# Masking the top-k scores with ScalarE's parametric ReLU, splitting the normalization, and transposing one turn sooner

## The chip, the cores and the metric

The kernel runs on one core of a Trainium2 chip. The core has a matrix engine (TensorE, PE in the profile, with its weight loads shown as PEld), a vector engine (VectorE, DVE), an activation engine (ScalarE, ACT), a general engine (GpSimd, POOL), and a queue that issues transfers (SyncE, SP). Each engine works through its own instructions in order; engines wait for each other through semaphores. The metric is the device time of one execution in microseconds (us).

## What is computed

An attention block with 8 batches, 8 heads, 576 positions and 64 columns a head, where each query keeps only its 32 largest scores, is followed by a SwiGLU feed-forward block on 4608 tokens of 512 columns with 1536 hidden columns. All is fp32.

```python
scores = scale * np.matmul(q, k.transpose(0, 1, 3, 2))          # scale = 1/8
kth = np.partition(scores, -top_k, axis=-1)[..., -top_k:-top_k + 1]
scores = np.where(scores >= kth, scores, -1000000000.0)
attn = np.exp(scores - np.max(scores, axis=-1, keepdims=True))
attn = attn / (np.sum(attn, axis=-1, keepdims=True) + 1e-09)
x = matmul(attn, v)                        # (B,H,S,D) -> (B*S, H*D)
g = x @ w_gate
out = (g * (1.0 / (1.0 + np.exp(-g))) * (x @ w_val)) @ w_out
```

## The kernel before

**Units and turns.** The attention work is cut into 160 units: batch (8), query tile (five, of 128 queries; the last has 64 queries of each head of a pair, stacked to 128 rows), and pair of heads (4). Units of the first four tiles handle two heads, [128 queries, 576 keys] each; units of the last tile hold both heads of the pair as one [128, 576] tile, and are half as much work. One pass of the main loop (L747) is called a turn; turn n carries out the selection of unit n on DVE and, around it, other steps of neighbouring units. A batch is 20 turns: 16 whole and 4 half ones.

**What happens to a unit.** `scores` (L278) multiplies q and k on PE into PSUM and copies the result to SBUF on ScalarE (`sc`, L313 or L299). `select` (L316) finds the 32 largest scores of each row on DVE: four rounds of `max` (eight values each, L328) with three `match_replace` between them (L332, which overwrites the values found, in `e`). That makes 14 instructions for two heads, which the text calls steps. Then L338 builds in `e` a penalty: (score < 32nd value) times a huge negative number. `penalize` (L342), on GpSimd, makes the bias from the largest value (L348) and adds the scores to the penalty (L350), one instruction a head. `weigh` (L353), on ScalarE, takes the exponential with the row sum as a by-product (L359) and adds 1e-9 to the sum (L364). `normalize` (L367) takes the reciprocal on DVE (L371) and multiplies each head by it on ScalarE (L374). `turn` (L376) transposes `e` on PE, nine blocks of up to 128 columns (L386), and copies them out on ScalarE (`et`, L387). The middle block of the nine holds columns of both heads. `values` (L398) multiplies by V on PE for two units at a time (L420) and copies the result into `xT` on ScalarE (L436).

**When.** In turn n: `penalize` and `weigh` of unit n-1; the reciprocal of n-1 at the turn's end, and its two multiplications at the beginning of turn n+1 (`scaled`); the transposes of unit n-2 (`TURN = 2`), behind up to two pieces of feed-forward work. In even turns the scores of units n+1 and n+2 are made and the V products of n-4 and n-3 (`scored` and `valued`, L708 and L713); the second score product is issued behind the V products, its copies behind `weigh`. In the first turns `rounding` works on the weights: a transfer, three ScalarE instructions (L114 to L117), one on DVE (L121) and two on GpSimd (L122, L123) for each of 36 pieces.

**Feed-forward work.** The tokens are taken in 18 blocks of 256 rows. A block may start when `values` has finished its rows for all four head pairs. `feed` (a generator) yields it in pieces: a piece of the first layer is four matrix products, eight records in the trace (L476), and costs 1; a piece of the second layer, three products (L562), costs 0.75. ScalarE evicts the gate (L501 to L503) and the value (L508), GpSimd multiplies them (L504, L509). From the second block on the second layer is done with seven products of quarters and additions on GpSimd (L548, L569 to L610). `share` (L694) gives each turn a credit: 6.4 pieces for a whole turn, less 0.7 for every unit whose scores or V products are made in it, less 0.6 for the transposes. `pieces(k)` issues up to k pieces if the credit lasts, at five places of the turn: 2 early, 1 and 1 around the middle, up to 6 at the end; what ScalarE and GpSimd owe for them is issued at the next `flush`.

**Order.** The last lines of the kernel tie each engine's instructions to the order in which the program wrote them. Nothing is rearranged: where one waits, all behind it on that engine wait. PSUM holds five banks for scores, V products and transposes (`ps_t`) and three for the feed-forward work.

```python
        if nxt:
            run(nxt.pop(0))
        if valued(n):
            finish_units(valued(n))
        if nxt:
            next(nxt[0])
        early[0]()
        if 0 <= n - 1 < NU:
            weigh(n - 1)
        if nxt:
            run(nxt.pop())
```

Of the kernel before, what the change touches and what calls it, by code (L numbers as in the profile page):

```python
# [8 lines left out]
AF = mybir.ActivationFunctionType  # L9
ALU = mybir.AluOpType  # L10
FP32 = mybir.dt.float32
# [4 lines left out]
P = 128  # L16
TOP_K = 32
LOWEST = -3.4028234663852886e38
FAR = -3.0e38
EPS = 1.0e-9  # L20
BLK = 256
WP = 256
# [3 lines left out]
def kernel(  # L26
# [66 lines left out]
    for i in range(NV):  # L93
        vt = consts.tile([P, P], FP32, name=f"vlast{i}")
        nc.vector.memset(vt[:], 0.0)
        vlast.append(vt)
    eps = consts.tile([P, 1], FP32, name="eps")
    nc.vector.memset(eps[:], EPS)
    wg = consts.tile([P, KC, DFF], FP32, name="wg")
    wv = consts.tile([P, KC, DFF], FP32, name="wv")  # L100
    wo = consts.tile([P, MC, DM], FP32, name="wo")
# [176 lines left out]
    def scores(n):  # L278
        b, qt, hp = units[n]
        slab = preps[b * NHP + hp]  # L280
        sc = work.tile([P, 2 * S], FP32, tag="sc", name="sc", bufs=3)
        halves = [slice(0, D), slice(D, P)]
        half = S // 2

        def bank():
            return ps_t.tile([P, 512], FP32, tag="t", name="s")


        if qt == J:
            banks = [bank() for _ in range(2)]  # L290
            for i, ps in enumerate(banks):
                for d in halves:
                    k0 = R + i * half
                    nc.tensor.matmul(  # L294
                        ps[d, 0:half], slab[d, S + R : S + 2 * R], slab[d, k0 : k0 + half]
                    )
            yield
            for i, ps in enumerate(banks):
                nc.scalar.copy(sc[:, i * half : (i + 1) * half], ps[:, 0:half])  # L299
        else:  # L300
            q0 = S + 2 * R + qt * P
            banks = []
            for i in range(2):
                for hh, d in enumerate(halves):
                    ps = bank()
                    banks.append((i + 2 * hh, ps))
                    k0 = (1 - hh) * R + i * half
                    nc.tensor.matmul(  # L308
                        ps[:, 0:half], slab[d, q0 : q0 + P], slab[d, k0 : k0 + half]
                    )  # L310
            yield
            for i, ps in banks:
                nc.scalar.copy(sc[:, i * half : (i + 1) * half], ps[:, 0:half])  # L313
        state[n] = dict(sc=sc)

    def select(n):  # L316

        nh = n_heads(units[n][1])
        sc = state[n]["sc"]
        m = small.tile([P, 2, TOP_K], FP32, tag="m", name="m", bufs=2)  # L320
        heads = [slice(t * S, (t + 1) * S) for t in range(nh)]
        e = work.tile([P, 2 * S], FP32, tag="e", name="e", bufs=3)
        state[n] |= dict(m=m, e=e, heads=heads)
# [2 lines left out]
        for r in range(rounds):  # L326
# [3 lines left out]
            if r < rounds - 1:  # L330
# [3 lines left out]
                    )  # L334
                    yield
                cur = e
        for t, hs in enumerate(heads):
            nc.vector.tensor_scalar(  # L338
                e[:, hs], sc[:, hs], m[:, t, TOP_K - 1 : TOP_K], FAR, ALU.is_lt, ALU.mult
            )  # L340

    def penalize(n):  # L342

        st = state[n]
        sc, m, e, heads = st.pop("sc"), st.pop("m"), st["e"], st["heads"]
        nh = len(heads)
        bias = small.tile([P, 2], FP32, tag="bias", name="bias")
        nc.gpsimd.tensor_scalar_mul(bias[:, 0:nh], m[:, 0:nh, 0], -scale)  # L348
        for hs in heads:
            nc.gpsimd.tensor_tensor(e[:, hs], e[:, hs], sc[:, hs], ALU.add)  # L350
        st["bias"] = bias

    def weigh(n):  # L353

        st = state[n]
        e, heads, bias = st["e"], st["heads"], st.pop("bias")
        tot = small.tile([P, 2], FP32, tag="tot", name="tot")
        for t, hs in enumerate(heads):
            nc.scalar.activation(  # L359
                e[:, hs], e[:, hs], AF.Exp, bias=bias[:, t : t + 1], scale=scale,  # L360
                accum_out=tot[:, t : t + 1],
            )
        nh = len(heads)
        nc.scalar.activation(tot[:, 0:nh], tot[:, 0:nh], AF.Identity, bias=eps[:])  # L364
        st["tot"] = tot

    def normalize(n):  # L367
        st = state[n]
        tot, e, heads = st.pop("tot"), st["e"], st.pop("heads")
        nh = len(heads)  # L370
        nc.vector.reciprocal(tot[:, 0:nh], tot[:, 0:nh])  # L371
        yield
        for t, hs in enumerate(heads):
            nc.scalar.mul(e[:, hs], e[:, hs], tot[:, t : t + 1])  # L374

    def turn(n):  # L376

# [329 lines left out]

    def scored(n):  # L708

        ahead = [n + 1] if n < 2 else [] if n % 2 else [n + 1, n + 2]  # L710
        return [m for m in ahead if m < NU]

    def valued(n):  # L713

        behind = [] if n % 2 else [n - 4, n - 3]
        return [m for m in behind if 0 <= m < NU]

    def pieces(n):
# [4 lines left out]
    def run(steps):  # L723
        for _ in steps:
            pass
# [15 lines left out]
    load(2)  # L741
    credit = [0.0]
    no = iter(())
    scaled = no
    TURN = 2
    due = [2.0]
    for n in range(NU + 3):  # L747
        nh = n_heads(units[n][1]) if n < NU else 1
# [17 lines left out]
            credit[0] = min(credit[0] + share(n), share(n) + 1)  # L766
        flush(on_act)
        if 0 <= n - 1 < NU:
            penalize(n - 1)
        flush(on_pool)  # L770
        run(scaled)
        if nxt:
            run(nxt.pop(0))
        if valued(n):
# [18 lines left out]
        flush(on_act)  # L793
        dve(1)
        dve(1)
        if 0 <= n - TURN < NU:
            run(turn(n - TURN))

        flush(on_pool)
        next(ahead, None)  # L800
        pieces(1)
        next(ahead, None)
        dve(1)
        pieces(1)
        dve(2, beside=False)
        run(topk)
        next(norm, None)
        scaled = norm
        pieces(6)
    while piece():  # L810
        pass
# [48 lines left out]
```

## Time and profile before

| | |
|---|---|
| median of 3 runs (lowest, highest) | 1791.11 us (1789.26, 1791.48) |
| the profiled execution | 1790.76 us, its span 1788.7 us |
| mean granted TensorE clock | 0.966 of full |
| L328 and L332, selection on DVE | 614.5 + 202.5 and 423.3 + 211.5 us |
| L338, penalty on DVE | 185.4 us, 288 instructions |
| L350, adding the scores on GpSimd | 408.7 us, 288 instructions, 1437 ns each |
| L359, exponential on ScalarE | 222.8 us, 288 instructions, 778 ns each |
| L374, normalization on ScalarE | 210.9 us, 288 instructions, 781 ns each |
| L386, transposes on PE | 184.0 us, idle before them 45.7 us |

A busy time is the union of an engine's instructions; "mean ns" is the length of one, which overlaps with its neighbour's. The slices cut the span into 40 equal parts and give each engine's busy share in tenths. Matrix products are pipelined and their ends are modelled, so a full PE need not be at its highest rate; its rate is read from the distance of one product to the next. In timelines a line gives start, length, engine, line, operation, operands (out<-in), number of instructions, and in brackets the idle time before it with what ended it.

### The profile page before, as it was taken

The page shows a single profiled execution, that of the slowest core. Times are in us where ns is not written, and L with a number is a line of the kernel's source. Part 1 is how long each engine was busy: PE and PEld are TensorE (multiplying, and loading weights), DVE is VectorE, ACT ScalarE, POOL GpSimd, SP SyncE. Part 2 cuts the span into 40 slices and gives each one's busy share as a digit, 9 for nine tenths or more (in the row PEclk, how much of TensorE's full clock was granted, in tenths as well). Part 3 has the DMA queues.
Part 4 walks back from the last instruction along what each step waited for, and adds up shares of the span by engine and source line. Part 5 has one row for each costly group of instructions (what it writes and reads, how often), then busy time and mean ns, then how long its engine had stood idle before and what let it go on. Part 6 is the DMA issues. An engine that isn't in the chain of part 4 may idle for free.

```text
span 1788.7 us, 30860 instructions
## 1 busy us (share of the span) xinstructions
PE 1686.3 (94%) x11012; PEld 1396.2 (78%) x11012; DVE 1619.7 (91%) x3372; ACT 1209.5 (68%) x2881; POOL 1068.0 (60%) x1058
## 2 busy tenths in 40 slices
PE   4458999799999999999999999999999999999999
PEld 3337678588888888888888878888888878888877
DVE  7999999999999999999999989999999999999400
ACT  6788776667667677667666776767676776676431
POOL 4878856455565646564656646566556555756434
PEclk7669999899999999999999999999999999999989
DMA  7433030001200030001200030000300020000000
GB/s 193 126 96 95 32 75 14 13 1 36 60 1 13 3 80 15 12 1 35 62 13 1 13 71 26 1 13 6 90 1 13 1 55 15 13 1 13 1 12 12
DMA packets 109306, 59.67 MB, mean 33 GB/s; under 512 B 88544, under 2 KB 96992, under 8 KB 109152
## 3 DMA queue, kind: packets, MB, share of 16 engines
q1 hardware_dynamic: 108016, 57.37, 12.3%
q8 instruction: 87, 1.43, 0.3%
q14 instruction: 67, 0.55, 0.1%
q10 hardware_dynamic: 1136, 0.33, 0.1%
HBM read 48.23 MB, written 9.44 MB: 32 GB/s over the span
## 4 chain that ended last, share of the span: by engine, by line
PE 81%; DVE 9%; POOL 4%; ACT 3%; issue 2%; DMA 0%; SPq 0%; POOLq 0%; ACTq 0%; DVEq 0%
PE f L476 39%; PE x_ps L562 9%; PE av L420 8%; PE s L308 7%; PE etps L386 6%; PE y_ps L562 6%; DVE m L328 4%; DVE e L332 4%; PE s L294 2%; POOL e L350 1%; PE kqps L263 1%; PE o_ps L522 1%; DVE e L338 1%; DVE size L121 1%; ACT e L359 1%
## 5 line engine op out<-in xcount | busy, mean ns | idle before, releaser
L328 DVE MAX8 m<-e 128x8 f32<-128x576 f32 x864 | 614.5, 746 | 3.3
L350 POOL TENSOR_TENSOR e<-e,sc 128x576 f32<-128x576 f32 x288 | 408.7, 1437 | 111.8 <-DVE e L338 53.8
L332 DVE MATCH_REPLACE8 e<-m,e 128x576 f32<-128x576 f32 x576 | 423.3, 741 | 0.0
L476 PE MATMUL f<-xT,wg 128*128 128x256 f32 x1728 | 405.6, 384 | 0.0
L476 PE MATMUL f<-xT,wv 128*128 128x256 f32 x1728 | 399.6, 380 | 0.0
L476 PEld LDWEIGHTS f<-xT,wg 128*128 128x128 f32 x1728 | 326.4, 192 | 52.2 <-issue 8.9
L476 PEld LDWEIGHTS f<-xT,wv 128*128 128x128 f32 x1728 | 323.0, 190 | 49.1 <-issue 7.9
L504 POOL TENSOR_TENSOR h<-h,half_g 128x512 f32<-128x512 f32 x108 | 139.0, 1287 | 284.1 <-ACT h L503 274.5
L359 ACT ACTIVATE e<-e,bias 128x576 f32<-128x576 f32 x288 | 222.8, 778 | 79.0 <-POOL e L350 79.0
L509 POOL TENSOR_TENSOR h<-h,val 128x512 f32<-128x512 f32 x108 | 139.4, 1291 | 148.7 <-ACT val L508 147.9
L386 PE MATMUL etps<-ident,e 128*128 128x128 f32 (+1 forms) x1312 | 184.0, 284 | 45.7 <-ACT e L374 37.5
L374 ACT ACTIVATE e<-e,tot 128x576 f32<-128x576 f32 x288 | 210.9, 781 | 20.9 <-DVE tot L371 20.8
L308 PE MATMUL s<-kqT 64*128 64x288 f32 x1024 | 181.4, 461 | 41.9 <-ACT sc L313 27.6
L386 PEld LDWEIGHTS etps<-ident,e 128*128 128x128 f32 (+1 forms) x1312 | 157.5, 145 | 76.6 <-ACT e L374 41.4
L387 ACT COPY et<-etps 128x512 f32<-128x512 f32 (+1 forms) x448 | 182.5, 483 | 44.1 <-PE etps L386 44.0
L332 DVE MATCH_REPLACE8 e<-m,sc 128x576 f32<-128x576 f32 x288 | 211.5, 740 | 0.0
L328 DVE MAX8 m<-sc 128x8 f32<-128x576 f32 x288 | 202.5, 739 | 9.1 <-ACT sc L313 9.1
L338 DVE TENSOR_SCALAR e<-sc,m 128x576 f32<-128x576 f32 x288 | 185.4, 680 | 1.1
L313 ACT COPY sc<-s 128x288 f32<-128x288 f32 x512 | 164.9, 407 | 17.0 <-PE s L308 16.8
L308 PEld LDWEIGHTS s<-kqT 64*128 64x128 f32 x1024 | 102.6, 198 | 89.6 <-ACT sc L313 33.0
L420 PE MATMUL av<-et,v 128*64 128x128 f32 (+1 forms) x2560 | 158.6, 267 | 0.0
L501 ACT ACTIVATE h<-f 128x512 f32<-128x512 f32 x108 | 64.3, 595 | 116.8 <-PE f L476 116.6
(73 smaller groups left out, 2045.9 us busy)
## 6 DMA issues: line engine op xcount, KB each, us to landing
v<-in_v_dram SPq DMA_DIRECT2D x32, 256.0 KB, 3.2
kq_in<-in_k_dram SPq DMA_DIRECT2D x63, 128.0 KB, 2.9
kq_in<-in_q_dram SPq DMA_DIRECT2D x63, 128.0 KB, 3.1
w<-in_moe_w_gate_dram SPq DMA_DIRECT2D x12, 512.0 KB, 3.9
w<-in_moe_w_val_dram SPq DMA_DIRECT2D x12, 512.0 KB, 3.7
w<-in_moe_w_out_dram SPq DMA_DIRECT2D x12, 512.0 KB, 3.6
out_dram<-o SPq DMA_DIRECT2D x38, 128.0 KB, 2.4
out_dram<-o SPq DMA_DIRECT2D x16, 256.0 KB, 2.4
```

The costliest lines, as they stand in the source:

```text
L308: nc.tensor.matmul(ps[:, 0:half], slab[d, q0 : q0 + P], slab[d, k0 : k0 + half])
L328: nc.vector.max(m[:, t, 8 * r : 8 * r + 8], cur[:, hs])
L332: nc.vector.match_replace(e[:, hs], m[:, t, 8 * r : 8 * r + 8], cur[:, hs], LOWEST)
L338: nc.vector.tensor_scalar(e[:, hs], sc[:, hs], m[:, t, TOP_K - 1 : TOP_K], FAR, ALU.is_lt, ALU.mult)
L350: nc.gpsimd.tensor_tensor(e[:, hs], e[:, hs], sc[:, hs], ALU.add)
L359: nc.scalar.activation(e[:, hs], e[:, hs], AF.Exp, bias=bias[:, t : t + 1], scale=scale, accum_out=tot[:, t : t + 1],)
L374: nc.scalar.mul(e[:, hs], e[:, hs], tot[:, t : t + 1])
L386: nc.tensor.transpose(ps[0:kl, c * P : (c + 1) * P], e[:, k0 : k0 + kl], ident[:])
L387: nc.scalar.copy(et[0:kl, c0 : c0 + cn, :], ps[0:kl, 0 : cn * P].rearrange("p (c j) -> p c j", c=cn),)
L420: nc.tensor.matmul(av[d, i, 0:ql], weights_, moving, start=c == (0 if last else J), stop=c == (J if last else J - 1),)
L476: nc.tensor.matmul(ps[:, i, :], w[:, kc, m * P : (m + 1) * P], x[:, kc, :], start=(kc == 0), stop=(kc == KC - 1),)
L562: nc.tensor.matmul(ps, lhsT, T[i][m], start=m == 0, stop=m == MQ - 1)
```

## The change

1. **Mask.** L338 and L350 go. Scores are scaled by 1/8 when they are copied from PSUM. In `weigh`, ScalarE applies a parametric ReLU to (32nd value - score): a kept score gives a value of zero or below, which is multiplied by 2^-90; a lower score stays as it is. The exponential then multiplies by -2^90, so that a kept score gives (score - 32nd value) and the others overflow to an exponential of zero. The bias is (32nd value - largest), one GpSimd subtraction in `shift`, where `penalize` was.
2. **Sum and normalization.** The addition of 1e-9 goes from ScalarE to DVE, one instruction of one column for each head, ahead of the reciprocal. The first head is multiplied on ScalarE, the second on GpSimd.
3. **Order.** `normalize` of unit n-1 is run whole in turn n, after the eighth of DVE's 14 steps, and the transposes of unit n-1 follow in the same turn (`TURN = 1`), behind up to four pieces of feed-forward work where they stood behind two. Scores of n+1 and n+2 and V products of n-3 and n-2 are made in odd turns; they were made in even turns.
4. `m` has three buffers in place of two.

```diff
-FAR = -3.0e38
+SMALL = 2.0**-90
...
-    eps = consts.tile([P, 1], FP32, name="eps")
-    nc.vector.memset(eps[:], EPS)
...
-                nc.scalar.copy(sc[:, i * half : (i + 1) * half], ps[:, 0:half])
+                nc.scalar.mul(sc[:, i * half : (i + 1) * half], ps[:, 0:half], scale)
...
-        m = small.tile([P, 2, TOP_K], FP32, tag="m", name="m", bufs=2)
+        m = small.tile([P, 2, TOP_K], FP32, tag="m", name="m")
...
-        for t, hs in enumerate(heads):
-            nc.vector.tensor_scalar(
-                e[:, hs], sc[:, hs], m[:, t, TOP_K - 1 : TOP_K], FAR, ALU.is_lt, ALU.mult
-            )
-
-    def penalize(n):
+
+    def shift(n):
 
         st = state[n]
-        sc, m, e, heads = st.pop("sc"), st.pop("m"), st["e"], st["heads"]
-        nh = len(heads)
+        m, nh = st["m"], len(st["heads"])
         bias = small.tile([P, 2], FP32, tag="bias", name="bias")
-        nc.gpsimd.tensor_scalar_mul(bias[:, 0:nh], m[:, 0:nh, 0], -scale)
-        for hs in heads:
-            nc.gpsimd.tensor_tensor(e[:, hs], e[:, hs], sc[:, hs], ALU.add)
+        nc.gpsimd.tensor_tensor(
+            bias[:, 0:nh], m[:, 0:nh, TOP_K - 1], m[:, 0:nh, 0], ALU.subtract
+        )
         st["bias"] = bias
 
     def weigh(n):
 
         st = state[n]
-        e, heads, bias = st["e"], st["heads"], st.pop("bias")
+        sc, m, e, heads, bias = st.pop("sc"), st.pop("m"), st["e"], st["heads"], st.pop("bias")
         tot = small.tile([P, 2], FP32, tag="tot", name="tot")
         for t, hs in enumerate(heads):
             nc.scalar.activation(
-                e[:, hs], e[:, hs], AF.Exp, bias=bias[:, t : t + 1], scale=scale,
+                e[:, hs], sc[:, hs], AF.Prelu, bias=m[:, t, TOP_K - 1 : TOP_K], scale=-1.0,
+                alpha=SMALL,
+            )
+        for t, hs in enumerate(heads):
+            nc.scalar.activation(
+                e[:, hs], e[:, hs], AF.Exp, bias=bias[:, t : t + 1], scale=-1.0 / SMALL,
                 accum_out=tot[:, t : t + 1],
             )
-        nh = len(heads)
-        nc.scalar.activation(tot[:, 0:nh], tot[:, 0:nh], AF.Identity, bias=eps[:])
         st["tot"] = tot
 
     def normalize(n):
         st = state[n]
         tot, e, heads = st.pop("tot"), st["e"], st.pop("heads")
         nh = len(heads)
+        for t in range(nh):
+            nc.vector.tensor_scalar_add(tot[:, t : t + 1], tot[:, t : t + 1], EPS)
         nc.vector.reciprocal(tot[:, 0:nh], tot[:, 0:nh])
         yield
         for t, hs in enumerate(heads):
-            nc.scalar.mul(e[:, hs], e[:, hs], tot[:, t : t + 1])
+            if t == 0:
+                nc.scalar.mul(e[:, hs], e[:, hs], tot[:, t : t + 1])
+            else:
+                nc.gpsimd.tensor_tensor(
+                    e[:, hs], e[:, hs], tot[:, t : t + 1].to_broadcast([P, S]), ALU.mult
+                )
...
-        ahead = [n + 1] if n < 2 else [] if n % 2 else [n + 1, n + 2]
+        ahead = [n + 1, n + 2] if n % 2 else [] if n else [1]
...
-        behind = [] if n % 2 else [n - 4, n - 3]
+        behind = [n - 3, n - 2] if n % 2 else []
...
-    scaled = no
-    TURN = 2
+    TURN = 1
...
-            penalize(n - 1)
+            shift(n - 1)
         flush(on_pool)
-        run(scaled)
...
         flush(on_act)
         dve(1)
         dve(1)
-        if 0 <= n - TURN < NU:
-            run(turn(n - TURN))
-
+        run(norm)
         flush(on_pool)
         next(ahead, None)
         pieces(1)
         next(ahead, None)
         dve(1)
         pieces(1)
+        if 0 <= n - TURN < NU:
+            run(turn(n - TURN))
         dve(2, beside=False)
         run(topk)
-        next(norm, None)
-        scaled = norm
         pieces(6)
```

## The prediction

> **What bounds the kernel now.** I read busy shares and slices first, then windows, then one pair of turns instruction by instruction. A turn is one unit's top-32 selection on DVE. The page:
>
> ```profile
> PE 1686.3 (94%) x11012; PEld 1396.2 (78%) x11012; DVE 1619.7 (91%) x3372; ACT 1209.5 (68%) x2881; POOL 1068.0 (60%) x1058
> ...
> PE   4458999799999999999999999999999999999999
> ...
> DVE  7999999999999999999999989999999999999400
> ```
>
> PE and DVE are both full from slice 5 on, but DVE stops two slices before the end and PE does not. PE's 102.4 us of idle lie almost all at the start, as the windows show:
>
> ```profile
> 906.99:917.55 10.56, 10.56 (x55) 9.35 (x55) 10.56 (x25) 7.06 (x15) 5.93 (x7) 1.00 0.23 51
> ...
> 0.00:137.00 137.00, 67.46 (x364) 46.90 (x364) 125.06 (x260) 102.23 (x227) 96.40 (x85) 0.68 0.51 139
> ```
>
> (Columns: width, then busy PE, PEld, DVE, ACT, POOL with counts, granted clock, DMA.) Before 137 us PE idles 69.5 us because no FFN block is ready; in mid-kernel a turn of 10.56 us leaves neither PE nor DVE a gap. Is that PE at its rate? The chain in order of time has FFN products in a long run at
>
> ```profile
> 1659.06 13.82 PE f L476 x64
> ```
>
> 0.216 us a record, and in turns at 3.62 us for 16, the same once the modelled end is off. So PE's work (one "piece" of 8 records, 1.73 us, is its unit) fixes the middle; DVE is a close second. Cutting DVE there shortens nothing by itself; idle put into PE lengthens everything.
>
> **The change part by part.** The profiled execution took 1790.76 us (span 1788.7), 0.35 below the median 1791.11; the sum is made against 1790.8.
>
> *DVE.* Out go 288 mask instructions, L338, by the view of that line (min/median/max):
>
> ```profile
> L338 DVE TENSOR_SCALAR e<-sc,m x288: 490/512/1611, 23.0 to 1696.9; 128x576 f32<-128x576 f32 x144
> ```
>
> 185.4 us busy, about 53 of it above 0.46 each, the step of a pair (0.92). In come two one-column adds per turn; DVE has no such row. The nearest is L371, 128x2, 0.155 us long and 0.07 to the next instruction; I take 0.35 us for adds plus reciprocal (bounds 0.15 and 0.7). A DVE turn goes from 10.56 to about 10.0. L338's maximum is a stall: its long ones end some 0.32 us after a GpSimd instruction ends. If the adds stalled alike, by the mean of 53/288 = 0.18 us, a pair's loop below would gain 0.4 and the whole some 20 us. The sum takes none, since L371, the nearer in size, never exceeds 0.178. The Trainium skill (VectorE: DVE Perf Modes, What auto-detection actually checks) takes an fp32 instruction into its two-port mode only where an outermost dimension longer than one is even or equal; L338's 576 columns fit that and a lone column has no such dimension, so by the page too the 20 us would be nothing. No run here shows it yet.
>
> *ScalarE.* Two Prelu per turn come in, priced as L359 (0.78 alone, 1.44 for a pair as L374 x2; bounds 0.68, L117's, and 0.97, with L359's accumulator read): +1.44. One multiply of two goes (1.44 to 0.78) and L364 (0.30). Net +0.5 a turn, about 70 us on 1209: still under 75%. The scaling in the score copy is free if as L502 (594 ns) beside L508's copy (586). The trace has one table load of 1.283 us, at the start, and the changed program's ScalarE order also holds one, so the sum has nothing for tables. A rule against the change: by the Trainium skill (ScalarE: Activation LUTs, What ACT_TABLE_LOAD costs) each switch to another set of functions takes some 2.66 us, and a Prelu outside the set of Exp would mean two a turn, an estimated 850 us; no page says where Prelu lies, and the order decides.
>
> *GpSimd.* L350's 408.7 us go; 128 multiplies with a broadcast come, priced as L350 (1.437; a broadcast addition in L548 is 1377 against 1288 for 512 columns, so up to 1.53): +190. L348 becomes one subtraction of the same size. GpSimd is not the bound, but this multiply now stands between the reciprocal and PE.
>
> *The shorter chain.* This decides. Before, unit n-1 is normalized at the end of turn n and transposed in turn n+1, so PE finds e ready (waits of PE on L374: 79 us in all, counting weight loads twice). After, all is in turn n, with transposes behind the first pieces. From the changed order I list PE between V products: scores, V (two units), scores, 5.2 us of FFN, transposes, 6.9, transposes, 3.4. The typical odd-even pair of turns is PE time 4.67 + 15.5 + 1.96 = 22.1.
>
> The same pair is now also a loop of waits, since every engine keeps its order. From a pair before, on PE's and ScalarE's timelines:
>
> ```profile
> 897.61 1.24 PE L308 MATMUL s<-kqT 64*128 64x288 f32 x8
> ...
> 901.11 1.24 PE L308 MATMUL s<-kqT 64*128 64x288 f32 x8
> ```
>
> ```profile
> 901.23 0.37 ACT L436 COPY xT<-av 128x256 f32<-128x256 f32 x1 [1.53 <-PE av L420]
> 901.50 0.78 ACT L359 ACTIVATE e<-e,bias 128x576 f32<-128x576 f32 x1
> ```
>
> Counted from the odd turn's first score product: V is copied out and ScalarE free at 3.9. The two Prelu stand behind that copy: +1.33 (0.66 from one start to the next), then both Exp with accumulators +1.68 (923.04 to 924.72) = 6.9. DVE has stood at its adds since: done at 7.25. Six of its 14 steps remain (912.53 to 916.63): 4.1, so the next turn begins at 11.35. Eight steps (906.99 to 912.53): 5.54, adds and reciprocal 0.35 = 17.25. GpSimd's multiply 1.5 = 18.75, the five transposes of the second head 0.6 = 19.35. Then PE's FFN behind the even transposes, and the next pair starts. So a pair lasts the greater of PE time and 19.35 + that last FFN: 22.8 in the typical pair against 22.1.
>
> Over the changed order's 59 full pairs from turn 10 on: 32 pairs have about 3.4 us at the end (+0.93 each, 29.9); 14 have 5.3, mostly pairs of the second-layer quarters, whose calls are shorter so that more of them fall behind (+1.96, 27.5); 13 have under 2 (+1.56, 20.3). Together 77.7 us of PE idle, in place of about 20 (102.4, less 75.1 before 203.8 us and 7.5 after 1700): +58.
>
> Who waits: behind DVE's adds stand six selection steps, and ScalarE's next Prelu behind those; behind PE's transposes stand FFN products and the next scores. DVE's 3 to 4 us of waiting per pair costs only through the loop. The even turn's ScalarE chain (1.33 + 1.68) is hidden by DVE's eight steps (5.54); without that cover it would add up to 3 us a pair. In odd turns ScalarE multiplies head 0 only after the second scores' copies (1.28) and a value or gate eviction (0.6 or 1.6): 9.6 to 10.6 against PE's arrival at 9.85; that can cost 0 to 0.8 a pair, and I take 0 in the sum, since it is mostly absorbed in the loop.
>
> *Half turns (one head).* In the second pair of each batch PE reaches the odd transposes at 5.7 (4.67 + 1.0 of k/q transposes) but e is ready at about 7.7: 2 us, six or seven times, +12.
>
> *Start.* V two units earlier lets the first FFN block begin in turn 9 rather than 10: -11.5. The loop at the half clock (0.68 granted) with weight rounding on ScalarE makes a pair there some 25.5 against 24.94 (11.46 + 13.48): +2.5. Net -9; bounds -19 (DVE's saving comes through fully) and 0.
>
> *DMA.* V loads of the next batch and each output store are issued one turn sooner; DMA is 1 to 18% busy after 200 us, so 0. The queues on SP have nothing late behind them. *Tail:* one turn less latency, -2 (0 to -4).
>
> Sum: 1790.8 + 58 + 12 - 9 - 2 = 1849.8; I say 1850.
>
> **The rivals.**
> *A, faster: the loop hides.* If its fixed part were 1.5 us shorter than 19.35, that is 17.85 (Prelu and Exp overlapping more, or DVE not held at the adds because V returns early), the same tally gives 22 us of idle, +2 net; half turns 0; start and DVE's saving -13 to -19: 1772 to 1782. For it: the start is DVE-bound, and DVE loses a tenth of its work there. Against: each link is a row of this trace, in engine order. The sign turns near 18.2.
> *B, slower still.* ScalarE's gate eviction before the multiply and GpSimd's hidden-layer products (1.29) before its multiply each delay e: another 1 us in the loop gives 132 us of idle: 1905. For it: in the changed GpSimd order a gate product or three 0.75 us subtractions often stand just ahead. Against: much is ready earlier.
> *C, no change.* PE's work is unchanged and full; start and stalls cancel: 1791, if the loop is 18.2.
>
> **How the numbers follow.** Chances: the loop as computed 0.56, B 0.25, A 0.15, C 0.04. From no change a measurement of this kernel tells about 0.2% (3.6 us). So faster 0.15, same 0.04, slower 0.81. Range 1782 (A's upper end) to 1905 (B); the forecast's own is 1820 to 1875 (loop 18.85 to 19.85 moves the tally by about 26 either way).
>
> **What would show it.** L338's and L350's groups gone; DVE at 85% or less, with a wait for the Exp line of some 150 us or more at its adds, mostly in odd turns; PE idle ahead of the transposes, released by GpSimd's multiply and ScalarE's, 60 to 110 us together; pairs of 22.8 instead of 21.1 to 22; first FFN product near 126 us; one table load. The prediction is wrong if PE is still without gaps in mid-kernel (A), if DVE's adds wait on nothing, or if the adds take over 0.5 us.

## The result and the profile after

The changed kernel took 1901.47 us (median of four runs, 1898.09 to 1904.70) where the kernel before, on the same chip, took 1791.30 (four runs, 1789.26 to 1792.04): 1.062 times as long, 95% interval 1.059 to 1.064. The forecast was 1850, so the direction was right and the size 51 us short. The profiled execution took 1898.96 us, 108.2 more than the profiled one of before.

The page of the changed kernel, busy time and two rows of slices:

```profile
PE 1707.3 (90%) x11012; PEld 1395.7 (74%) x11012; DVE 1483.0 (78%) x3371; ACT 1273.1 (67%) x2881; POOL 787.1 (41%) x898
...
PE   4449899798999999999999989999999989898999
...
DVE  6786778897898878887888877888888878887410
```

DVE and GpSimd lost 137 and 281 us of work, and the kernel got longer. PE has the same 11012 products, its row is broken by eights, and its idle time went from 102.4 to 189.9 us. DVE's row has almost no nines left: it waits for others.

Where the time lies is read from windows. I cut both executions at the first selection step of unit 20 and of unit 156, so that each stage holds the same selections. First before, then after (width, then busy PE, PEld, DVE, ACT, POOL with counts, granted clock, DMA):

```profile
0.00:242.20 242.20, 166.98 (x949) 121.07 (x950) 226.55 (x457) 186.25 (x421) 175.96 (x151) 0.80 0.38 106
242.20:1646.10 1403.90, 1384.19 (x9315) 1159.38 (x9314) 1366.08 (x2866) 974.89 (x2360) 827.26 (x838) 0.99 0.09 23
1646.10:1788.70 142.60, 135.13 (x752) 115.72 (x750) 27.10 (x53) 48.35 (x101) 64.76 (x69) 0.96 0.04 11
```

```profile
0.00:276.69 276.69, 178.04 (x1031) 128.98 (x1032) 201.68 (x454) 198.01 (x432) 149.00 (x139) 0.79 0.35 95
276.69:1768.55 1491.86, 1408.70 (x9332) 1163.55 (x9331) 1257.07 (x2865) 1030.23 (x2363) 584.34 (x698) 0.99 0.09 22
1768.55:1897.20 128.65, 120.51 (x653) 103.20 (x651) 24.22 (x55) 44.85 (x90) 53.78 (x61) 0.97 0.04 9
```

The start got 34.5 us longer, the middle 88.0, the end 14.0 shorter. In the middle PE's idle went from 19.7 to 83.2 us (width less busy). Its busy time rose by 24.5 for 17 more products; some of that is idle too, since the modelled end of a product before a gap counts as busy. The list of waits says who waits for whom (engine, tile, line, then what was waited for; us in all, times, longest):

```profile
POOL e L376 <- DVE tot L370: 415.9, 98, 12.0
DVE tot L369 <- ACT e L358: 320.1, 170, 10.3
...
PE etps L390 <- ACT e L374: 133.4, 59, 7.8
```

The same view for the middle stage alone:

```profile
PE etps L390 <- ACT e L374: 62.3, 43, 7.2
PE etps L390 <- POOL e L376: 13.0, 4, 4.1
```

L369 are the additions of 1e-9 on DVE, L358 the exponential, L374 and L376 the multiplications on ScalarE and GpSimd, L390 the transposes. DVE stands at its additions until the exponential ends, and PE stands at the transposes until the multiplication ends.

One typical pair of turns, 977.70 to 1000.41, from the timeline (start, length, engine, line, operation):

```profile
977.70 1.24 PE L306 MATMUL s<-kqT 64*128 64x288 f32 x8
...
981.32 0.37 ACT L440 COPY xT<-av 128x256 f32<-128x256 f32 x1 [0.71 <-PE av L424]
981.59 1.44 ACT L353 ACTIVATE e<-sc,m 128x576 f32<-128x576 f32 x2
982.93 0.76 ACT L358 ACTIVATE e<-e,bias 128x576 f32<-128x576 f32 x1
...
984.58 0.15 DVE L369 TENSOR_SCALAR tot<-tot 128x1 f32<-128x1 f32 x1 [0.60 <-ACT e L358]
...
988.94 1.41 DVE L326 MAX8 m<-sc 128x8 f32<-128x576 f32 x2
...
994.92 0.78 ACT L374 ACTIVATE e<-e,tot 128x576 f32<-128x576 f32 x1 [1.05 <-DVE tot L370]
995.06 1.15 POOL L376 TENSOR_TENSOR e<-e,tot 128x576 f32<-128x576 f32 x1 [5.76 <-DVE tot L370]
995.75 1.27 PE L390 MATMUL etps<-ident,e 128*128 128x128 f32 x9
...
996.86 1.89 PE L480 MATMUL f<-xT,wg 128*128 128x256 f32 x8
...
1000.41 0.99 PE L306 MATMUL s<-kqT 64*128 64x288 f32 x5
```

This is the loop of the prediction, link by link: from the first score product to the parametric ReLU 3.89 us (3.9 forecast), to the exponential 5.23 (5.23), to the next turn 11.24 (11.35), to the first feed-forward product behind the even transposes 19.16 (19.35), then 3.55 of feed-forward work, 22.71 in all.

The three lines' own views (shortest, median, longest in ns):

```profile
L369 DVE TENSOR_SCALAR tot<-tot x288: 140/153/156, 33.6 to 1826.8; 128x1 f32<-128x1 f32 x144
...
L353 ACT ACTIVATE e<-sc,m x288: 757/782/837, 31.4 to 1825.0; 128x576 f32<-128x576 f32 x144
...
L376 POOL TENSOR_TENSOR e<-e,tot x128: 1144/1147/1338, 34.9 to 1773.0; 128x576 f32<-128x576 f32 x128
```

### The profile page after: what moved, and what is told of

Its sections match the earlier page's. It is cut to its first block, busy times and chain, and to the rows that moved or that the text cites. A ratio compares the mean times of both kernels' runs of the same rounds, so it can differ in the third digit from the quotient of the medians.

```text
span 1897.2 us, 30998 instructions
## 1 busy us (share of the span) xinstructions
PE 1707.3 (90%) x11012; PEld 1395.7 (74%) x11012; DVE 1483.0 (78%) x3371; ACT 1273.1 (67%) x2881; POOL 787.1 (41%) x898
## 4 chain that ended last, share of the span: by engine, by line
PE 61%; DVE 16%; ACT 15%; issue 4%; POOL 3%; SPq 1%; DMA 0%; ACTq 0%; POOLq 0%; DVEq 0%
PE f L480 29%; PE av L424 9%; DVE m L326 7%; DVE e L330 7%; PE etps L390 6%; PE s L306 5%; PE x_ps L566 5%; ACT e L358 4%; PE y_ps L566 3%; ACT e L353 2%; ACT e L374 2%; PE s L292 2%; ACT sc L311 1%; ACT xT L440 1%; PE o_ps L526 1%
## 5 line engine op out<-in xcount | busy, mean ns | idle before, releaser
L480 PE MATMUL f<-xT,wg 128*128 128x256 f32 x1728 | 401.4, 382 | 0.0
L376 POOL TENSOR_TENSOR e<-e,tot 128x576 f32<-128x576 f32 x128 | 147.9, 1155 | 449.1 <-DVE tot L370 415.9
L390 PE MATMUL etps<-ident,e 128*128 128x128 f32 (+1 forms) x1312 | 191.4, 292 | 155.1 <-ACT e L374 133.4
L390 PEld LDWEIGHTS etps<-ident,e 128*128 128x128 f32 (+1 forms) x1312 | 156.3, 148 | 198.0 <-ACT e L374 166.8
L391 ACT COPY et<-etps 128x512 f32<-128x512 f32 (+1 forms) x448 | 184.4, 480 | 164.3 <-PE etps L390 164.3
L369 DVE TENSOR_SCALAR tot<-tot 128x1 f32<-128x1 f32 x288 | 39.3, 150 | 320.3 <-ACT e L358 320.1
L358 ACT ACTIVATE e<-e,bias 128x576 f32<-128x576 f32 x288 | 220.6, 773 | 9.0 <-POOL bias L341 6.2
L353 ACT ACTIVATE e<-sc,m 128x576 f32<-128x576 f32 x288 | 211.1, 783 | 0.0
L311 ACT ACTIVATE sc<-s 128x288 f32<-128x288 f32 x512 | 167.7, 413 | 59.7 <-PE s L306 59.1
L306 PE MATMUL s<-kqT 64*128 64x288 f32 x1024 | 172.9, 448 | 17.4 <-ACT et L391 8.5
L374 ACT ACTIVATE e<-e,tot 128x576 f32<-128x576 f32 x160 | 125.7, 785 | 78.0 <-DVE tot L370 77.8
L513 POOL TENSOR_TENSOR h<-h,val 128x512 f32<-128x512 f32 x108 | 138.1, 1279 | 83.2 <-ACT val L512 81.2
L424 PEld LDWEIGHTS av<-et,v 128*64 128x64 f32 x2560 | 139.9, 142 | 7.1 <-issue 3.0
```

The source lines that it names most:

```text
L306: nc.tensor.matmul(ps[:, 0:half], slab[d, q0 : q0 + P], slab[d, k0 : k0 + half])
L311: nc.scalar.mul(sc[:, i * half : (i + 1) * half], ps[:, 0:half], scale)
L353: nc.scalar.activation(e[:, hs], sc[:, hs], AF.Prelu, bias=m[:, t, TOP_K - 1 : TOP_K], scale=-1.0, alpha=SMALL,)
L358: nc.scalar.activation(e[:, hs], e[:, hs], AF.Exp, bias=bias[:, t : t + 1], scale=-1.0 / SMALL, accum_out=tot[:, t : t + 1],)
L390: nc.tensor.transpose(ps[0:kl, c * P : (c + 1) * P], e[:, k0 : k0 + kl], ident[:])
L391: nc.scalar.copy(et[0:kl, c0 : c0 + cn, :], ps[0:kl, 0 : cn * P].rearrange("p (c j) -> p c j", c=cn),)
```

## The experiments

The theory: the new order closes a loop through ScalarE, DVE and PE, and that alone costs the time; the new mask and the split are worth a little. Rivals: the parametric ReLU's load on ScalarE, GpSimd's multiplication or its queue, or something in the start. Kernels without an interval below ran once or twice, so differences of a few us between them mean little. All times of the kernel before, beside these runs, had medians between 1790.1 and 1791.9 us. "Pairs" below are my tally of pairs of whole turns from the trace, from one first score product to the next, some 50 in a kernel; their median was 22.38 us before and 22.73 after.

**Mask and split, in the order of before.** Against the changed kernel:

```diff
-        ahead = [n + 1, n + 2] if n % 2 else [] if n else [1]
+        ahead = [n + 1] if n < 2 else [] if n % 2 else [n + 1, n + 2]
...
-        behind = [n - 3, n - 2] if n % 2 else []
+        behind = [] if n % 2 else [n - 4, n - 3]
...
-    TURN = 1
+    scaled = no
+    TURN = 2
...
         flush(on_pool)
+        run(scaled)
...
-        run(norm)
+        if 0 <= n - TURN < NU:
+            run(turn(n - TURN))
...
-        if 0 <= n - TURN < NU:
-            run(turn(n - TURN))
         dve(2, beside=False)
         run(topk)
+        next(norm, None)
+        scaled = norm
```

> The new mask and the new split of the normalization with the order of before: scores and V in even turns, the reciprocal at the turn's end, multiplications in the next turn, transposes of n-2. Theory of the closed loop (it is the order that costs, because normalization and transposes of n-1 stand in turn n): 1765 to 1795 us, PE idle before the transposes under 20 us in all, DVE at some 1480 us busy, the start as in the kernel before or shorter. Rival of ScalarE's load (its 211 us of Prelu are what slows): 1870 us or more. Rival of GpSimd (its multiply of the second head is late for PE): 1820 to 1860, with PE waiting for that multiply.

Measured: 1776.65 us, 0.9928 of before (0.9911 to 0.9944). It beats both kernels. Page, the row of the middle stage, and list of waits:

```profile
PE 1677.0 (95%) x11012; PEld 1387.6 (78%) x11012; DVE 1488.3 (84%) x3371; ACT 1264.2 (71%) x2881; POOL 782.9 (44%) x898
```

```profile
230.28:1631.19 1400.91, 1378.14 (x9307) 1153.15 (x9306) 1260.18 (x2865) 1020.66 (x2361) 585.69 (x702) 1.00 0.09 23
```

```profile
PE etps L390 <- ACT e L374: 28.6, 9, 5.4
```

All the operations of the change are in it, ScalarE is busier than in the changed kernel by share (71%), and PE hardly waits. So neither the parametric ReLU's load nor the split costs the time; the order does: 1901.5 against 1776.7. The stages show where 14.5 us are gained: start 230.3 us instead of 242.2, middle 1400.9 instead of 1403.9, end 143.2 instead of 142.6. DVE's turn is shorter by half a microsecond, and still the middle gains almost nothing.

**Only the new order, with the old mask and normalization.** Against the kernel before (`m` has the third buffer here too):

```diff
-        m = small.tile([P, 2, TOP_K], FP32, tag="m", name="m", bufs=2)
+        m = small.tile([P, 2, TOP_K], FP32, tag="m", name="m")
...
-        ahead = [n + 1] if n < 2 else [] if n % 2 else [n + 1, n + 2]
+        ahead = [n + 1, n + 2] if n % 2 else [] if n else [1]
...
-        behind = [] if n % 2 else [n - 4, n - 3]
+        behind = [n - 3, n - 2] if n % 2 else []
...
-    TURN = 2
+    TURN = 1
...
-        run(scaled)
...
+        run(norm)
...
+        if 0 <= n - TURN < NU:
+            run(turn(n - TURN))
         dve(2, beside=False)
         run(topk)
-        next(norm, None)
-        scaled = norm
```

> The new order with the mask and the normalization of before: penalty on DVE (L338) and GpSimd, both heads multiplied on ScalarE. Loop theory: the loop is 6.9 less 1.33 for the two Prelu plus 0.3 for the addition on ScalarE, 4.1 + 0.9 for the rest of the turn with the penalty, 5.54 and the reciprocal, 1.44 and 0.98 on ScalarE and PE: some 19.2 us, so about as slow as the change, 1880 to 1930 us. Rival of ScalarE's load and rival of GpSimd's multiply: neither is here, so about 1791 us.

Measured: 1890.79 us, and the same wait:

```profile
PE etps L386 <- ACT e L374: 126.1, 57, 8.2
```

The order alone costs 100 us; the third buffer is not it, as the run above has it too. In the new order, the new mask and split cost another 8 (1898.96 profiled, against this one run); in the old order they gain 14.

**Parametric ReLU and exponential ahead of the V products,** and so of the weights' rounding too. Against the changed kernel:

```diff
             run(nxt.pop(0))
+        if 0 <= n - 1 < NU:
+            weigh(n - 1)
         if valued(n):
             finish_units(valued(n))
...
         early[0]()
-        if 0 <= n - 1 < NU:
-            weigh(n - 1)
```

> The change, with Prelu and Exp issued ahead of the V products and of the weights' rounding in the turn. Loop theory: in odd turns Prelu no longer waits for V's copy, the loop loses some 1.5 to 2 us, and most of what was added in whole turns goes: 60 to 80 us off there, and the start gains too (rounding and V no longer ahead of Prelu): 1800 to 1840 us. Rival of ScalarE's load: the same instructions, so within 10 us of 1900. Rival of GpSimd: the same, within 10 us.

Measured: 1826.24 us. V's products and their copy were links of the loop; ScalarE keeps its order, so one line moved past them takes 72.7 us (profiled runs) off. The typical pair is back at 22.38, PE's own time. Of the 72.7, 23.4 came from the start (253.3 us), where rounding was passed as well, and 51.8 from the middle (1440.1), where V alone was: rounding's last instruction ended at 202.1 us. The middle is still 36 us longer than before, and PE waits 37.2 us there at the transposes for ScalarE's multiplication; what makes up this rest was not tested.

**Both heads multiplied on ScalarE.** Against the changed kernel:

```diff
-            if t == 0:
-                nc.scalar.mul(e[:, hs], e[:, hs], tot[:, t : t + 1])
-            else:
-                nc.gpsimd.tensor_tensor(
-                    e[:, hs], e[:, hs], tot[:, t : t + 1].to_broadcast([P, S]), ALU.mult
-                )
+            nc.scalar.mul(e[:, hs], e[:, hs], tot[:, t : t + 1])
```

> The change, with both heads multiplied on ScalarE. Loop theory: GpSimd's 1.15 us and ScalarE's 0.78 stand side by side, a pair on ScalarE takes 1.44 and stands behind the score copies in odd turns: 5 to 30 us slower, 1905 to 1930 us. Rival of GpSimd: its multiply is what PE waits for, so 20 to 50 us faster. Rival of ScalarE's load: some 100 us more work on ScalarE, 1920 to 1990 us.

Measured: 1897.97 us, no change, a miss for every theory. The pairs show two effects that cancel: the typical pair went from 22.73 to 22.95, as the second multiplication stands behind the first, and the longest pair fell from 29.8 to 26.4.

**The second head on DVE**, made to see GpSimd's part by itself:

```diff
-                nc.gpsimd.tensor_tensor(
-                    e[:, hs], e[:, hs], tot[:, t : t + 1].to_broadcast([P, S]), ALU.mult
-                )
+                nc.vector.tensor_scalar(
+                    e[:, hs], e[:, hs], tot[:, t : t + 1], None, ALU.mult
+                )
```

> The changed kernel with the second head multiplied on DVE (one instruction, 128x576, in place of GpSimd's). GpSimd then stands in no chain from the selection to the transposes. Queue theory: in place of GpSimd's 1.15 us and whatever additions stand ahead of it, the loop gets DVE's multiply twice (once before the six steps, once before the transposes), 2 x 0.5 less 1.15, so the typical pair moves by less than 0.3 us, and the pairs of 25 to 30 us that waited for GpSimd go: 10 to 35 us off 1899, 1865 to 1890, no PE wait at the transposes from GpSimd. Rival, that GpSimd's queue costs nothing in sum: 1890 to 1905. Rival, that DVE's new two-port instructions stall behind GpSimd as L338's did, by up to 1.1 us: over 1905.

Measured: 1912.72 us, slower than the theory asked for, and in the number nearest to the last rival; but the timeline gives another reason. In the typical pair:

```profile
1021.26 0.52 DVE L376 TENSOR_SCALAR e<-e,tot 128x576 f32<-128x576 f32 x1
...
1031.84 0.78 ACT L374 ACTIVATE e<-e,tot 128x576 f32<-128x576 f32 x1 [1.20 <-DVE tot L370]
1032.67 1.21 PE L390 MATMUL etps<-ident,e 128*128 128x128 f32 x9 [0.66 <-ACT e L374]
```

The 0.52 us that DVE's multiplication takes in the odd turn delays the next turn, its reciprocal and ScalarE's multiplication of the first head, and the typical pair went from 22.73 to 23.26: +0.53, the loop's arithmetic to the hundredth. My expectation had subtracted GpSimd's 1.15, but ScalarE's multiplication ends a transposition later all the same; the two were tied. The stall exists (L376 on DVE had a median of 520 ns and a longest of 1397, a mean of 570), but 128 x 0.05 = 6.4 us of it is the smaller part. The other half of the expectation held: the three longest pairs of the changed kernel, 29.74, 29.80 and 29.21, became 23.82, 26.73 and 25.04. Over 55 pairs the mean rose by 0.19, 10 of the 14 us. What GpSimd's queue costs is seen in one of the three, on PE's and GpSimd's timeline of the changed kernel:

```profile
1636.98 0.73 POOL L552 TENSOR_TENSOR o<-o,p 128x256 f32<-128x256 f32 x1
1637.48 0.60 PE L390 MATMUL etps<-ident,e 128*128 128x128 f32 x4
1637.66 1.27 POOL L552 TENSOR_TENSOR p<-p,p 128x512 f32<-128x512 f32 x1
1638.89 2.09 POOL L614 TENSOR_TENSOR h<-h,xT 128x256 f32<-128x256 f32 x3
1640.94 1.15 POOL L376 TENSOR_TENSOR e<-e,tot 128x576 f32<-128x576 f32 x1
1642.14 1.33 PE L390 MATMUL etps<-ident,e 128*128 128x128 f32 x5 [4.06 <-POOL e L376]
```

Additions of the second layer stand ahead of the multiplication, and PE stands for 4.06 us between the first head's transposes and the second's.

**Transposes behind all feed-forward pieces of the turn.** Against the changed kernel:

```diff
-        if 0 <= n - TURN < NU:
-            run(turn(n - TURN))
         dve(2, beside=False)
         run(topk)
         pieces(6)
+        if 0 <= n - TURN < NU:
+            run(turn(n - TURN))
```

> The change, with the transposes of n-1 behind all FFN pieces of the turn, not ahead of the last ones. Loop theory: a pair lasts the greater of PE time, 22.1, and 19.35 plus the FFN behind the even transposes, now nothing: whole pairs fall from 22.7 to some 22.1 and the quarter pairs from 24.4 to 22, 50 to 75 us off in whole and half turns, the start as it was: 1825 to 1850 us. Rival (the length of the chain itself, wherever the transposes stand, or the extra ScalarE work, sets the pair): within 15 us of 1899.

Measured: 1896.34 us; the expectation failed. The pairs say why. Nine of the pairs that had lasted 22.69 to 22.71 did lose by it, and last 22.38 to 22.44, PE's own time; those of 22.73 stayed at 22.73, and needed the exponential ahead of V to come down. And pairs of the second-layer quarters grew: six pairs lasted 26.6 to 30.0, and in four of them PE waited 3.6 to 4.1 us once, each time on GpSimd: on the multiplication in the pairs that begin at 1625.7 and 1726.6, on second-layer additions (L614, L586) in those that begin at 634.4 and 1496.8. One queue of GpSimd serves both, and whichever comes second is late.

**Exponential ahead of V and transposes last,** both edits together:

> e3_weigh_first with the transposes behind all FFN pieces of the turn. Theory of two loops of nearly one length (one through the even transposes and the FFN behind them, one through Exp behind V, ScalarE's multiplication and the odd transposes), each of which e7 and e3 alone left standing: with both cut, the stretch from turn 20 to 156 falls from 1440 us to 1400 to 1420, the whole to 1790 to 1810. Rival (what transposes last leaves standing is GpSimd's queue, where the second layer's additions and the multiplication wait for each other): no gain on e3, 1815 to 1830, with PE waiting for GpSimd's additions.

Measured: 1826.25 us, the same as with the exponential ahead alone. The typical pair was at PE's 22.38 already, so there was nothing for the second edit to take. The time is the rival's. PE's wait on GpSimd at the transposes is only 6.2 us here, against 9.5 with the one edit; two long pairs of 27.3 and 29.3 have 2.9 and 2.8 of it. But in the middle PE also waits 16.6 us at second-layer products (L566) for GpSimd's additions, against 2.6 with the one edit, as the rival said. The rest of this kernel's excess in the middle (1452 us against 1403.9) I have not settled.

**Rounding of the weights later,** behind the exponential and the second score copies. Three kernels: the changed one, mask and split in the old order, and the exponential ahead of V (there `weigh` stands further up already, so that only the copies are passed):

```diff
-        early[0]()
         if 0 <= n - 1 < NU:
             weigh(n - 1)
         if nxt:
             run(nxt.pop())
+        early[0]()
```

> The change, with the weights' three ScalarE instructions of each piece (and the wait for its transfer) issued behind Prelu, Exp and the score copies in place of ahead of them. It tests what held up the start. Theory (rounding stands between V's copy and Prelu, 1.7 us and at times a transfer's wait in each odd turn): the start of turn 10 moves from 155.7 to 135 to 145 us, the whole 1880 to 1892 us, the middle as it was. Rival (V at the half clock alone makes the start slow): turn 10 within 3 us of 155.7, the whole within 5 us of 1899.

> e1_order_back with the weights' ScalarE instructions behind Prelu, Exp and the score copies. PE is full in the middle, so only the first 14 turns can move: 0 to 8 us less than e1, 1768 to 1777 us. If ScalarE paces nothing there: 1776 as e1.

> The changed kernel with both parametric ReLU and exponential ahead of the V products (as in the run that had 1826) and, besides, the weight rounding behind them. It measures the start. Theory that the early loop is V's copy (at the half clock) and the rounding's three ScalarE instructions between a score and its exponential: both gone, so turn 10 at 125 to 133 us in place of 136.0 and 155.7, and turn 20 at 240 to 250 in place of 253.3 and 276.7; in all 1815 to 1823. Rival, that rounding is not in this loop once the exponential goes first: within 3 us of 1826, or longer if the rounding then delays the weights.

Measured: 1892.97, 1787.00 (0.998 of before, 0.997 to 0.9989) and 1828.37 us. Only the first has its sign: unit 10's selection began at 147.9 us instead of 155.7, less than I expected, and the kernel was 6 shorter. In the second the start got 10 us longer (DVE idle in the first 14 turns 12.9 us instead of 5.6), in the third unit 10 began at 138.8 instead of 136.0. So the rounding is a small link of the new order's early loop, some 8 us by turn 10, and none in the other two. In the second and third kernels the last rounded weights came later, at 195.5 us instead of 187.7 and at 206.0 instead of 202.1 (the end of L121); that this is what lengthened them is not shown.

**Only the normalization one turn sooner.** The order of before, with additions, reciprocal and multiplications in the middle of turn n. Against the kernel with mask and split in the old order:

```diff
         flush(on_pool)
-        run(scaled)
...
         dve(1)
+        run(norm)
         if 0 <= n - TURN < NU:
             run(turn(n - TURN))
...
         run(topk)
-        next(norm, None)
-        scaled = norm
```

> As e1_order_back, but the adds, the reciprocal and the multiplications stay in turn n after DVE's eighth step, as in the change; transposes, scores and V products are where they were before. Loop theory: PE is no longer in the loop (it transposes n-2), so DVE waits at its adds without holding PE: 1775 to 1805 us, the excess over e1 all in the first 14 turns, where DVE paces. Rival (the early normalization is itself what costs, through DVE's wait): 1850 us or more, with DVE's wait for Exp near the 320 us of the change.

Measured: 1843.17 us, between the theories, and my own failed: with the transposes still a turn later I thought nobody would wait. The list of waits, of the whole execution, names those who do:

```profile
DVE tot L369 <- ACT e L358: 264.1, 151, 13.3
...
ACT e L374 <- DVE tot L370: 111.3, 71, 3.6
...
PE s L306 <- ACT et L391: 49.0, 12, 10.2
```

DVE waits for the exponential, ScalarE's multiplication waits for DVE's reciprocal, behind it on ScalarE stand the copies out of the transposes' banks (L391), and PE's next scores wait for these banks. It is the same kind of loop, closed at another place. Four waits of the last line, 35.3 us of it, lie before 140 us; in the middle PE waits 27.4 us for L391, half at the scores and half at the transposes of k and q (L261). **With those copies ahead of the normalization** it should open:

```diff
-        run(norm)
         if 0 <= n - TURN < NU:
             run(turn(n - TURN))
+        run(norm)
```

> As e5_norm_early_only, with the transposes of n-2 and their copies (L391) issued ahead of the adds, the reciprocal and the multiplications. In e5 PE waited 49 us at scores for L391's copies, which stand on ScalarE behind a multiplication that waits for DVE. Theory (the loop had closed again through ScalarE's order and the PSUM banks that those copies free): the stretch from turn 20 to turn 156 falls from 1455 us to 1400 to 1420, the whole to 1775 to 1810. Rival (DVE's wait for Exp behind V is enough to hold the pace): 1830 to 1850, as e5.

Measured: 1815.62 us, some 6 us outside the theory's range. The middle went from 1454.7 to 1429.0 us, so about half of the 53.8 by which it stood above 1400.9 was that queue: PE's waits for L391 in the middle fell from 27.4 us to 7.7. In the whole execution one of them is still long,

```profile
PE s L306 <- ACT et L391: 34.3, 7, 8.8
```

but 30.4 us of it are four waits before 137 us, in the start. Of the 28 us left in the middle, PE waits 18.5 at second-layer products for GpSimd's additions, where mask and split in the old order had 1.4; why they come late, and the rest, is not settled.

## Why the prediction was right, and where it was short

*The number.* The direction and the mechanism were right; the sum was 51 us short (by the profiled runs 43.5 in the start and 18 in the middle, less 12 at the end). That 1901 still lies in the range is luck in part: 1905 was rival B's end, a loop longer by 1 us in every pair, and the typical pair was not longer than forecast. The start, which had been given bounds of -19 and 0, filled the distance.

*What bounds.* Right. Mask and split in the old order took DVE's work in the middle from 1366 to 1260 us and the middle's length from 1403.9 to 1400.9 only: PE, 98% busy there, fixes it, and idle put into PE made the kernel longer. Of the rivals, A (the loop hides) needed a fixed part below 18.2 us, and C (no change) one of 18.2; it was 19.16.

*DVE, ScalarE, GpSimd's prices.* Additions and reciprocal took 0.32 us in an even turn (0.35 forecast), a whole DVE turn without waits 9.95 (10.0). The additions never stalled: 156 ns at most, against L338's 1611. DVE's 576-column multiplication in the experiment had 1397 at most. That fits the Trainium skill (VectorE: DVE Perf Modes, What auto-detection actually checks), whose two-port mode asks for an outermost dimension longer than one that is even or equal: 576 columns have it and a lone column does not. No run shows the mode itself. The parametric ReLU took 782 ns (0.78), and the trace has one table load, as the order said, so the Trainium skill's price for table switches (ScalarE: Activation LUTs, What ACT_TABLE_LOAD costs) was not paid. GpSimd's multiplication was the one price missed: 1.147 us, not 1.437 to 1.53, which changes little, since ScalarE's 0.78 for the first head and nine transposes end at about the same time.

*The loop of waits.* Right to 0.2 us in its links: 19.16 for 19.35, and pairs of 22.7 where 22.8 was forecast. What was mis-sized is PE's own time, which the loop has to exceed: 22.38 for the typical pair, not 22.1, so that such a pair lost 0.35 us and not 0.7. But the 112 whole turns of the middle took 77.9 us more (1229.4 to 1307.3), 1.4 a pair: most of the loss is in longer pairs. That the tally, which charged nearly every pair 0.9 to 2 us, came near is therefore partly luck. PE's idle ahead of the transposes, released by ScalarE and GpSimd, was 62.3 + 13.0 = 75.3 us in the middle; in the whole execution it was 153.3, where 60 to 110 was forecast, as the start had as much again. DVE was 78% busy (85 or less forecast) and waited 320 us for the exponential (150 or more). The runs that shorten the loop (1826) and lengthen it by a known 0.52 (pair +0.53) confirm it in both directions; with the transposes last it opened in nine pairs only.

*The middle as a sum.* +70 was forecast, 58 and 12, and +88 came. PE's idle there was not what was short: it grew by 63.5 us. What the sum lacked is the 24.5 us by which PE's busy time grew. Part of that is the clock, which fell after long idles, as the last section shows: in the middle it was 0.50 or 0.51 in eight stretches of together 44.5 us, 34.6 of them busy, where the kernel before had three of 17.1 us, 12.9 busy. At half the rate that loses an estimated 10.8 us of work, half of the difference. The same 1260 second-layer products lasted 295.0 us (289.8 before). The 17 further products and the modelled ends of products ahead of gaps are in the 24.5 too; they were not measured apart.

Rival B's mechanism, GpSimd's queue, was left out of the sum, and it was real in a few pairs: three pairs of 29.2 to 29.8 stand 88.75 - 3 x 24.65 = 14.8 us above what the tally gave a pair with 5.3 us at its end, and with DVE's multiplication in GpSimd's place those pairs fell to 23.8 to 26.7. These stalls are part of the idle, of which PE waited 13.0 us for GpSimd's multiplication.

*The start.* This is the mis-sized term: -9 forecast (bounds -19 and 0), +34.5 measured, and the first feed-forward product at 147.1 us, where 126 was forecast and 141.4 was before. An early pair was put at 25.5 us; turns 5 and 6, from one first score product to the next, lasted 29.67. The lines of the timeline from 79.58 on show the links that I had sized by mid-kernel rows:

```profile
79.71 0.67 ACT L112 ACTIVATE size<-w 128x512 f32<-128x512 f32 x1 [4.71 <-DMA w<-in_moe_w_gate_dram]
...
83.41 0.69 PE L424 MATMUL av<-et,vlast 128*64 128x128 f32 x4
...
87.98 0.37 ACT L440 COPY xT<-av 128x256 f32<-128x256 f32 x1 [3.92 <-PE av L424]
88.25 0.68 ACT L112 ACTIVATE size<-w 128x512 f32<-128x512 f32 x1
...
89.93 1.42 ACT L353 ACTIVATE e<-sc,m 128x576 f32<-128x576 f32 x2
...
92.14 0.15 DVE L369 TENSOR_SCALAR tot<-tot 128x1 f32<-128x1 f32 x1 [6.27 <-ACT e L358]
...
94.76 2.18 PE L390 MATMUL etps<-ident,e 128*128 128x128 f32 x9 [5.66 <-ACT e L374]
```

V's products take 4.45 us to the next score product (83.41 to 87.86) at a granted clock of 0.51 in that stretch (0.65 is the mean of the first 137 us), where mid-kernel they take 2.33 (978.87 to 981.20, clock 1.00); three rounding instructions add 1.7 (88.25 to 89.93); and ScalarE had stood 4.71 us for a weight transfer. With the exponential ahead of V and of the rounding, turns 5 and 6 lasted 24.3 us, and the start lost 23.4 of its 34.5. Moving the rounding alone, and with it ScalarE's wait for the weights, took 7.6 off the start (269.1 us). So V is the main link, rounding and the wait for the weights together the smaller one; these two were not tested apart.

*Half turns.* +12 forecast; 32 half turns took 253.0 us before and 269.0 after, +16, of which the four of the last batch, in the end, have 3.6.

*The end.* -2 forecast, -14 measured: 653 products of PE are left after unit 156's selection begins, where 752 were left before. A start and a middle held up elsewhere had already done 99 of them; it is no gain of its own.

## What to carry to other kernels

Before a step is moved to an earlier turn, walk once around the ring that it closes through all in-order engines (who waits for it, and what stands behind that wait on the same queue); when the ring's fixed part plus whatever an engine issues behind its last link is longer than the bounding engine's own time, each such turn pays the difference. Price each link at the stage in which it runs, because the same link may take twice as long in the start. A change that joins an operation's substitution with a new order is best tried apart: here the first gained 0.7% and the second cost 6%.

## What the runs showed of the hardware that was not expected

After a few microseconds of idle PE's granted clock was half for a few more. In the pair above, after the idle of 4.06 us, and after one of 3.89 at 1160.3, in windows of the changed kernel (clock is the number before the DMA share):

```profile
1642.10:1645.83 3.73, 3.69 (x12) 3.15 (x13) 2.34 (x6) 2.59 (x6) 0.87 (x2) 0.50 0.01 2
```

```profile
1161.46:1166.50 5.04, 5.04 (x14) 4.03 (x14) 2.36 (x8) 3.70 (x8) 0.72 (x1) 0.51 0.00 0
1166.50:1171.60 5.10, 5.10 (x25) 4.51 (x24) 5.10 (x11) 1.26 (x2) 2.38 (x2) 1.00 0.27 103
```

Twelve second-layer products took 5.2 us where they take 2.75, so that such a wait costs about 6.4 us and not 4. After an idle of 2.81 us the clock was 1.00 at one place (898.3) and 0.64 at another (1110.7). The Trainium skill (TensorE: Matmul & The Clock Gate, Why this matters for your kernels) warns of gaps above some 3 us; the runs agree, and show that a somewhat shorter one can be followed by it too.

On GpSimd the multiplication with a [128, 1] column broadcast as second operand was cheaper than the addition of two tensors of the same 576 columns: 1.147 us against L350's 1.437.
